# Attention block with a gated unit on one core: order of the first q/k products, pieces of the output weights, engines of the last rows

## The chip, the cores and the metric

The kernel runs on one core of a Trainium2 chip. The metric is the device time of one execution in microseconds; lower is better. The core has a matrix engine (TensorE, PE in the profile, with its weight loads as PEld), VectorE (DVE), ScalarE (ACT), GpSimd (POOL) and SyncE (SP), each with its own instruction stream, executed in order, and 16 DMA engines. Here SP issues nearly all transfers, POOL a few.

## The reference

x is [1, 2048, 576]; there are 32 heads of 18 columns; the gated unit is 4608 wide. All is float32.

```python
xn  = (x - mean(x)) / sqrt(var(x) + 1e-5)
q, k, v = split_heads(xn @ wqkv)                       # 576 -> 3 x 576
s   = (softmax(q @ k.T / sqrt(18)) @ v) @ wo           # heads joined, 576 -> 576
b   = ((xn @ w_gate) * (xn @ w_up)) @ w_down           # 576 -> 4608 -> 576
out = x + s * silu(b)
```

## The kernel before

A float32 operand is split into a high part (a copy in the matrix engine's own 32-bit type, made by ACT) and a low part (operand minus high part, made by DVE or POOL). A product sums high x high, high x low and low x high. The depth of 576 is 4 blocks of 128 and one of 64; in a weight tile the places 0 to 3 and 8 are high, 4 to 7 and 9 are low, and the 64-row rests of high and low share place 8. `PAIRS` lists, for one output bank, the 14 matmuls as (weight place, data place):

```python
PAIRS = ([(i, i) for i in range(4)] + [(i, 4 + i) for i in range(4)]
         + [(8, 8)] + [(4 + i, i) for i in range(4)] + [(9, 8)])
```

In q/k blocks and in the output product the pairs mean different things: in `qk_block` the first number is a piece of the weights and the second one of x; in the output product the first is also a piece of the weights (`wos`), the second one of the transposed attention output (`oT`).

The kernel has three stages. They share one instruction order, which the program writes out by hand.

*Start (to about 200 us).* x comes in chunks of 512 rows. `first_columns` handles chunk 0 tile by tile (128 rows): `norm_stats` and `norm_apply` normalise on DVE (L338 to L349; ACT takes the square root at L340 and copies the last 64 columns at L356), `turn` transposes on TensorE (L400, L401) and ACT writes the high part (L402), `lows` writes the low part on DVE (L406). `w_split` splits the weights: ACT copies (L127), POOL subtracts (L131). POOL's first subtraction is held behind the last `norm_apply` of chunks 0 and 1 by a dependence that the kernel adds (`behind`). Then `qk_block` runs 9 blocks of 128 output columns for each chunk (L441, evicted at L444 and L445), and `v_block` makes v.

*Middle (to about 2530 us).* A planner with costs and due times interleaves the score products (L644, L695), the product with v (L706), the gate and up products (L748) and the down product (L799) on the two halves of the array. It prepares the output weights on the side (`wo_split`, stored to `swo`). When the last gate product is issued, `wo_fetch` loads them: the tile `wos` (places 0 to 7, in a buffer of the x chunks) at L935 and `wos2` (places 8 and 9, in a buffer of the gate weights) at L937.

*End.* For each of 16 tiles of 128 rows: `fetch_o` loads the attention output (`oin`, L1324), `fetch` loads the gate rows (`gin`, L1331, for the first 12 tiles) and x (`xi`, L1333). `join` copies 64 columns on ACT (L1349), `columns` transposes on TensorE (L1357, L1359) and splits with ACT (L1361, L1363) and DVE (L1362, L1364); 28 matmuls make the two halves of the output (L1380); DVE multiplies each half by the gate (L1390), POOL adds x (L1391) and POOL stores the whole tile (L1394). The first four tiles' `oin` are fetched ahead of the loop, then their `gin` and `xi`; tile i + 4 is fetched during tile i. The gate rows of the last four tiles are finished during the loop in small pieces (`chore`; L883 to L893).

SP executes its transfers in order. Each waits for its own buffer to be free and, since eight completion semaphores are used in turn, for the transfer eight places earlier to have landed. In the buffers of the end stage, the second `oin` tile lies where the middle stage kept a tile that the down product reads.

Of the kernel before, what the change touches and what calls it, by code (L numbers as in the profile page):

```python
# [14 lines left out]
try:  # L15
# [5 lines left out]
FT = mybir.dt.float32  # L21
# [3 lines left out]
OP = mybir.AluOpType  # L25
# [4 lines left out]

PAIRS = ([(i, i) for i in range(4)] + [(i, 4 + i) for i in range(4)]
         + [(8, 8)] + [(4 + i, i) for i in range(4)] + [(9, 8)])


def _run(gen):
# [5 lines left out]
def kernel(  # L41
# [10 lines left out]
    nc = tc.nc  # L52
# [26 lines left out]
    swo = dram.tile([128, 10, D], FT, name="swo")  # L79
# [3 lines left out]
    def bank(tag, bufs, k=None):  # L83
        if tag == "g":
            if k is None:
                k = turns[0] = (turns[0] + 1) % 4
            return psum.tile([128, 512], FT, name="pg", tag=f"g{k}", bufs=1)
        return psum.tile([128, 512], FT, name="p" + tag, tag=tag, bufs=bufs)
# [7 lines left out]
    out2 = out.rearrange("o s d -> (o s) d")  # L96
# [246 lines left out]
    def norm_apply(c, t):  # L343
        if t == 0:
            xns[c] = ep.tile([128, 4, 640], FT, name="xn", bufs=1)
        xn = xns[c]
        mv, rs = stat.pop((c, t))
        nc.vector.reciprocal(rs[:, 1:2], rs[:, 0:1])
        op = nc.vector.tensor_scalar(xn[:, t, 0:D], xin[c][:, t, :], mv[:, 0:1], rs[:, 1:2],  # L349
                                     op0=OP.subtract, op1=OP.mult)  # L350
        if c < 2 and t == 3:
            behind.append(op)
        if c:
            nc.vector.tensor_copy(xn[:, t, D:640], xn[:, t, 512:D])
        else:
            nc.scalar.activation(xn[:, t, D:640], xn[:, t, 512:D], AF.Copy)  # L356
# [35 lines left out]
    def first_columns():  # L392

        xc = xcs[0] = pp.tile([128, 9, 512], FR, name="xcx", bufs=2)
        ps, last = {}, bank("a", 2)

        def turn(t):
            ps[t] = bank("g", 3).rearrange("p (k s) -> p k s", k=4)
            for k in range(4):
                nc.tensor.transpose(ps[t][:, k, :], xns[0][:, t, k * 128:(k + 1) * 128], ident)  # L400
            nc.tensor.transpose(last[:, t * 128:(t + 1) * 128], xns[0][:, t, 512:640], ident)  # L401
            nc.scalar.activation(xc[:, 0:4, t * 128:(t + 1) * 128], ps[t], AF.Copy)  # L402

        def lows(t):
            cs = slice(t * 128, (t + 1) * 128)
            nc.vector.tensor_tensor(xc[:, 4:8, cs], ps[t], xc[:, 0:4, cs].bitcast(FT), op=OP.subtract)  # L406

        norm_stats(0, 0)
        norm_stats(0, 1)
        norm_apply(0, 0)  # L410
        norm_stats(0, 2)
        turn(0)
        wq[0], todo = w_split(raws[0], 2)
        for f, a in todo[:2]:
            f(*a, rest=False)
        norm_apply(0, 1)
        norm_stats(0, 3)
        turn(1)
        norm_apply(0, 2)
        lows(0)  # L420
        norm_apply(0, 3)
        for f, a in todo[:2]:
            f(*a, high=False)
        turn(2)
        lows(1)
        turn(3)
        nc.scalar.activation(xc[:, 8, :], last, AF.Copy)
        for f, a in todo[2:]:
            f(*a)
        lows(2)  # L430
        lows(3)
        nc.vector.tensor_tensor(xc[64:128, 8, :], last[64:128, :], xc[64:128, 8, :].bitcast(FT), op=OP.subtract)
        xns.pop(0)


    def qk_block(b, c):
        w = wq[b // 2][:, b % 2]
        p = bank("a" if nqk[0] % 2 else "b", 2)
        nqk[0] += 1
        for n, (a, e) in enumerate(PAIRS):  # L440
            nc.tensor.matmul(p, w[:, a, :], xcs[c][:, e, :], start=n == 0,  # L441
                             stop=n == len(PAIRS) - 1)
        hl = pp.tile([128, 2, 512], FR, name="hl", bufs=3)
        nc.scalar.activation(hl[:, 0, :], p, AF.Copy)  # L444
        nc.vector.tensor_tensor(hl[:, 1, :], p, hl[:, 0, :].bitcast(FT), op=OP.subtract)  # L445
        g0 = blocks[b]
        for kind in range(2):
            lo, hi = max(g0, kind * D), min(g0 + 128, (kind + 1) * D)
            if lo < hi:
                dst = sqk[kind, :, lo - kind * D:hi - kind * D, c * 512:(c + 1) * 512]  # L450
                nc.sync.dma_start(dst.rearrange("h r s -> r h s"), hl[lo - g0:hi - g0].bitcast(FT))
# [149 lines left out]
    n = 8  # L601
# [24 lines left out]
    with ExitStack() as mid:  # L626
# [278 lines left out]
        wos = {}  # L905
# [26 lines left out]

        def wo_fetch():
            wos[0] = xcp.tile([128, 8, D], FR, name="wos", tag="xc")
            nc.sync.dma_start(wos[0].bitcast(FT), swo[:, 0:8, :])  # L935
            wos[1] = wpool.tile([128, 2, D], FR, name="wos2", tag="wgu", bufs=2)
            nc.sync.dma_start(wos[1].bitcast(FT), swo[:, 8:10, :])  # L937

        passed = {}

# [377 lines left out]
    with ExitStack() as end:  # L1318
        ep = end.enter_context(tc.tile_pool(name="end", bufs=1, reuse_waits="tile"))
        oin, gin, xi = {}, {}, {}  # L1320

        def fetch_o(t):
            oin[t] = ep.tile([128, 640], FT, name="oin", bufs=5)
            nc.sync.dma_start(oin[t][:, 0:D], so[t * 128:(t + 1) * 128, :])  # L1324

        def fetch(t):
            rows = slice(t * 128, (t + 1) * 128)
            ready(sdone, t)
            if t < 12:
                gin[t] = ep.tile([128, D], FT, name="gin", bufs=5)  # L1330
                nc.sync.dma_start(gin[t], sg[rows, :])  # L1331
            xi[t] = ep.tile([128, D], FT, name="xi", bufs=5)
            nc.sync.dma_start(xi[t], x2[rows, :])  # L1333

        order = list(range(NT))
        for t in range(12, NT):
            def end_silu(e, t=t):
                gin[t] = e
                sdone.add(t)

            silu(t, lambda: ep.tile([128, D], FT, name="gl", bufs=4), end_silu)
        for t in order[:4]:
            fetch_o(t)
        for t in order[:4]:
            fetch(t)
        oT = {}

        def join(t):
            nc.scalar.activation(oin[t][:, D:640], oin[t][:, 512:D], AF.Copy)  # L1349

        def columns(t):
            o = oin.pop(t)
            oc = ep.tile([128, 9, 128], FR, name="oT", bufs=2)
            oT[t] = oc
            p = bank("b", 2)
            for k in range(4):
                nc.tensor.transpose(p[:, k * 128:(k + 1) * 128], o[:, k * 128:(k + 1) * 128], ident)  # L1357
            p2 = bank("a", 2)
            nc.tensor.transpose(p2[:, 0:128], o[:, 512:640], ident)  # L1359
            pf = p.rearrange("p (k s) -> p k s", k=4)  # L1360
            nc.scalar.activation(oc[:, 0:4, :], pf, AF.Copy)  # L1361
            nc.vector.tensor_tensor(oc[:, 4:8, :], pf, oc[:, 0:4, :].bitcast(FT), op=OP.subtract)  # L1362
            nc.scalar.activation(oc[:, 8, :], p2[:, 0:128], AF.Copy)  # L1363
            nc.vector.tensor_tensor(oc[64:128, 8, :], p2[64:128, 0:128],  # L1364
                                    oc[64:128, 8, :].bitcast(FT), op=OP.subtract)

        join(order[0])
        join(order[1])
        columns(order[0])
        for i, t in enumerate(order):  # L1370
            if i + 2 < NT:
                join(order[i + 2])
            if i + 1 < NT:
                columns(order[i + 1])
            oc = oT.pop(t)
            ps = [bank("g", 3), bank("g", 3)]
            for h in range(2):
                for n, (a, e) in enumerate(PAIRS):
                    w = wos[0][:, a, :] if a < 8 else wos[1][:, a - 8, :]
                    nc.tensor.matmul(ps[h][:, 0:HALF], oc[:, e, :], w[:, h * HALF:(h + 1) * HALF],  # L1380
                                     start=n == 0, stop=n == len(PAIRS) - 1)
            if i + 4 < NT:
                fetch_o(order[i + 4])
                fetch(order[i + 4])
            y = ep.tile([128, D], FT, name="y", bufs=2)
            g = gin.pop(t)
            xt = xi.pop(t)
            for h in range(2):
                cs = slice(h * HALF, (h + 1) * HALF)
                nc.vector.tensor_tensor(y[:, cs], ps[h][:, 0:HALF], g[:, cs], op=OP.mult)  # L1390
                nc.gpsimd.tensor_tensor(y[:, cs], y[:, cs], xt[:, cs], op=OP.add)  # L1391
            for _ in range(3):
                chore()
            nc.gpsimd.dma_start(out2[t * 128:(t + 1) * 128, :], y)  # L1394


# [26 lines left out]
```

## Time and profile before

| what | value |
|---|---|
| median of 3 runs | 2619.4 us (2617.34 to 2620.2) |
| profiled execution | 2617.51 us |
| its span, first to last instruction | 2615.7 us |
| mean granted TensorE clock | 0.999 |
| TensorE, DVE, ACT, POOL busy | 99%, 69%, 60%, 27% |
| DMA moved | 434.30 MB, 166 GB/s |

A timeline row gives the start in us, the time it took, the engine, the line, the operation, the tiles (written <- read), how many instructions were merged into the row, and, in brackets, how long the engine had been idle before it and what ended that. SPq and POOLq are the instruction queues of SP and POOL: there a transfer's row shows its issue, not its transport.

### The profile page before, as it was taken

Reading aid. Unit: us, or ns where it says so; the run is one execution under the profiler, and the core shown is the slowest. Engines: PE = TensorE matmul, PEld = TensorE weight load, DVE = VectorE, ACT = ScalarE, POOL = GpSimd, SP = SyncE. Lnnn points to the kernel's source line nnn. Section 1 sums busy time; section 2 is a strip of 40 time slices with the busy share of each in tenths; the row PEclk is TensorE's granted clock in tenths of the full one; section 3 lists DMA queues with packets and bytes.
Section 4 is the critical chain, followed back from the end, with each engine's and each line's share of the span. In section 5 each row is a group of like instructions: output and inputs, shape, how many; then the busy total and the mean of one; then the engine's idle time right before and its main releaser. Section 6 shows DMA issues by size and latency. Waiting matters only on the chain.

```text
span 2615.7 us, 59267 instructions
## 1 busy us (share of the span) xinstructions
PE 2597.6 (99%) x24504; PEld 2126.2 (81%) x24504; DVE 1797.8 (69%) x2978; ACT 1569.2 (60%) x3125; POOL 696.1 (27%) x738
## 2 busy tenths in 40 slices
PE   8999999999999999999999999999999999999998
PEld 7899888777788878877788788777887788888878
DVE  7209667777777777776777777776777777777336
ACT  4224567666766666666666666665666566666641
POOL 3114444434431222212131222121221222111115
PEclk9999999999999999999999999999999999999999
DMA  7799777676663435564564444444454454443355
GB/s 244 233 296 259 211 205 194 179 192 191 181 184 120 146 134 158 156 168 147 154 164 120 137 146 142 139 134 137 147 168 132 134 151 142 146 134 119 122 188 189
DMA packets 201390, 434.30 MB, mean 166 GB/s; under 512 B 81216, under 2 KB 130784, under 8 KB 167584
## 3 DMA queue, kind: packets, MB, share of 16 engines
q1 hardware_dynamic: 196672, 415.18, 53.1%
q0 software_dynamic: 4448, 15.34, 1.9%
q8 instruction: 192, 3.15, 0.5%
q14 instruction: 78, 0.64, 0.1%
HBM read 314.64 MB, written 110.56 MB: 163 GB/s over the span
## 4 chain that ended last, share of the span: by engine, by line
PE 98%; DMA 1%; DVE 1%; ACT 0%; issue 0%; SPq 0%; POOL 0%; POOLq 0%; ACTq 0%
PE pg L748 35%; PE pg L706 17%; PE pg L799 16%; PE pa L644 11%; PE pb L695 8%; PE pb L441 2%; PE pg L1380 2%; PE pg L498 2%; PE pa L441 2%; DMA xc<-sx 1%; DMA oin<-so 0%; PE pa L695 0%; PE pb L1357 0%; DVE mx L646 0%; PE pg L381 0%; DMA xin<-in_A_x_dram 0%
## 5 line engine op out<-in xcount | busy, mean ns | idle before, releaser
L646 DVE TENSOR_REDUCE mx<-pa 128x1 f32<-128x512 f32 x2016 | 1354.1, 686 | 313.4 <-PE pa L644 181.5
L697 ACT ACTIVATE pt<-pb 128x512 f32<-128x512 f32 x2003 | 1153.9, 601 | 515.5 <-PE pb L695 381.9
L748 PE MATMUL pg<-xc,wgu 64*128 64x512 f32 x7776 | 1389.9, 392 | 0.6 <-DMA xc<-sx 0.5
L748 PEld LDWEIGHTS pg<-xc,wgu 64*128 64x128 f32 x7776 | 1053.2, 186 | 55.2 <-issue 1.7
L799 PE MATMUL pg<-wd,hs 64*128 64x288 f32 x6816 | 823.8, 293 | 0.0
L644 PE MATMUL pa<-ks,qs 54*128 54x512 f32 x2016 | 789.0, 398 | 0.2 <-DVE mx L646 0.2
L799 PEld LDWEIGHTS pg<-wd,hs 64*128 64x128 f32 x6816 | 773.2, 185 | 12.6 <-issue 2.5
L695 PE MATMUL pb<-qs,ks 56*128 56x512 f32 x2003 | 782.7, 398 | 0.0
L706 PE MATMUL pg<-pt,vt 128*32 128x512 f32 x4096 | 459.4, 594 | 1.1 <-ACT st L856 0.6
L644 PEld LDWEIGHTS pa<-ks,qs 54*128 54x128 f32 x2016 | 366.4, 184 | 77.5 <-issue 59.7
L779 POOL TENSOR_TENSOR hs<-us,hs 128x512 fp32r<-128x512 f32 x144 | 186.0, 1292 | 907.8 <-ACT hs L766 658.1
L695 PEld LDWEIGHTS pb<-qs,ks 56*128 56x128 f32 x2003 | 363.4, 184 | 7.6 <-ACT pt L697 0.6
L826 POOL TENSOR_TENSOR acc<-acc,st 128x288 f32<-128x288 f32 x293 | 236.0, 810 | 498.2 <-ACT st L856 255.5
L706 PEld LDWEIGHTS pg<-pt,vt 128*32 128x32 f32 x4096 | 123.3, 110 | 277.4 <-issue 268.6
L712 DVE TENSOR_TENSOR oc<-oc,pg 128x512 f32<-128x512 f32 x64 | 44.0, 687 | 292.6 <-PE pg L706 292.6
L249 POOL TENSOR_TENSOR wgu<-wraw,wgu 128x384 fp32r<-128x384 f32 x108 | 108.4, 1014 | 228.0 <-ACT wgu L248 131.7
L856 ACT ACTIVATE st<-pg 128x288 f32<-128x288 f32 x293 | 120.6, 412 | 25.8 <-PE pg L799 18.7
L862 DVE TENSOR_TENSOR acc<-acc,pg 128x288 f32<-128x288 f32 x252 | 112.7, 448 | 32.5 <-PE pg L799 30.1
L761 DVE TENSOR_TENSOR us<-pg,us 128x512 f32<-128x512 f32 x144 | 98.4, 683 | 27.7 <-PE pg L748 25.4
L754 ACT ACTIVATE us<-pg 128x512 f32<-128x512 f32 x144 | 86.6, 601 | 40.6 <-PE pg L748 26.7
L710 ACT ACTIVATE oc<-pg 128x512 f32<-128x512 f32 x32 | 19.1, 598 | 136.7 <-PE pg L706 136.7
L766 ACT ACTIVATE hs<-us 128x512 fp32r<-128x512 f32 x144 | 90.6, 629 | 12.2 <-DVE us L761 12.0
(128 smaller groups left out, 1266.9 us busy)
## 6 DMA issues: line engine op xcount, KB each, us to landing
wgu<-swg SPq DMA_DIRECT2D x102, 1152.0 KB
wd<-swd SPq DMA_DIRECT2D x50, 1152.0 KB
swg<-wgu SPq DMA_DIRECT2D x36, 1152.0 KB
qs<-sqk SPq DMA_DIRECT2D x192, 144.0 KB
ks<-sqk SPq DMA_DIRECT2D x192, 144.0 KB
swd<-wd SPq DMA_DIRECT2D x18, 1152.0 KB
sqk<-hl SPq DMA_DIRECT2D x32, 512.0 KB
wraw<-in_B_w_up_dram SPq DMA_DIRECT2D x36, 288.0 KB
```

The source lines that it names most:

```text
L249: nc.gpsimd.tensor_tensor(w[:, 9 + b:12 + b, :], raw[:, b:b + 3, :], w[:, b:b + 3, :].bitcast(FT), op=OP.subtract)
L644: nc.tensor.matmul(p, q[rows, t * 128:(t + 1) * 128], k[rows, c * 512:(c + 1) * 512], start=True, stop=True)
L646: nc.vector.tensor_reduce(mx[h][:, t, c:c + 1], p, axis=AX.X, op=OP.max)
L695: nc.tensor.matmul(p, k[rows, t * 128:(t + 1) * 128], q[rows, c * 512:(c + 1) * 512], start=True, stop=True)
L697: nc.scalar.activation(pt[t, c // 2][:, c % 2, :], p, AF.Exp, scale=scale)
L706: nc.tensor.matmul(p[32 * c:32 * c + 32, :], vt[h // 2][:, t, 6 * (h % 2):6 * (h % 2) + 32], pt[t, c // 2][:, c % 2, :], start=t == ts[0], ...
L748: nc.tensor.matmul(ps, gw[n][half[r], a, :], xg[i][half[r], e, :], start=k == 0, stop=k == len(TERMS) - 1)
L779: nc.gpsimd.tensor_tensor(hj[:, 1, :], h32, hj[:, 0, :].bitcast(FT), op=OP.subtract)
L799: op = nc.tensor.matmul(ps[:, 0:HALF], hs[u][half[r], j, a, s * 128:(s + 1) * 128], dw[u][half[r], j, e, i * HALF:(i + 1) * HALF], start=( ...
L826: nc.gpsimd.tensor_tensor(a, a, st, op=OP.add)
L856: nc.scalar.activation(st, ps[:, 0:HALF], AF.Copy)
L862: nc.vector.tensor_tensor(a, a, ps[:, 0:HALF], op=OP.add)
```

## The change

It has three parts. In `qk_block` the pairs are taken in another order: high x high, then low weights x high x, then high weights x low x with the shared place 8, then place 9; and in `first_columns` the last tile is normalised before the first tile's low part is written. The output weights are loaded in three transfers: places 0 to 3 where all were loaded before, then the first two `oin` tiles, then places 8 and 9 and places 4 to 7, then the next two `oin` tiles. For the last tile, DVE adds x to each half and SP stores each half by itself; the other 15 tiles are unchanged. The order of pairs in the output product and in v stays as it is.

```diff
+QK_PAIRS = PAIRS[0:4] + PAIRS[9:13] + PAIRS[4:9] + PAIRS[13:14]
...
         norm_apply(0, 2)
+        norm_apply(0, 3)
         lows(0)
-        norm_apply(0, 3)
...
-        for n, (a, e) in enumerate(PAIRS):
+        for n, (a, e) in enumerate(QK_PAIRS):
             nc.tensor.matmul(p, w[:, a, :], xcs[c][:, e, :], start=n == 0,
-                             stop=n == len(PAIRS) - 1)
+                             stop=n == len(QK_PAIRS) - 1)
...
         def wo_fetch():
             wos[0] = xcp.tile([128, 8, D], FR, name="wos", tag="xc")
-            nc.sync.dma_start(wos[0].bitcast(FT), swo[:, 0:8, :])
+            nc.sync.dma_start(wos[0][:, 0:4, :].bitcast(FT), swo[:, 0:4, :])
             wos[1] = wpool.tile([128, 2, D], FR, name="wos2", tag="wgu", bufs=2)
+
+        def wo_rest():
             nc.sync.dma_start(wos[1].bitcast(FT), swo[:, 8:10, :])
+            nc.sync.dma_start(wos[0][:, 4:8, :].bitcast(FT), swo[:, 4:8, :])
...
-        for t in order[:4]:
+        for t in order[:2]:
+            fetch_o(t)
+        wo_rest()
+        for t in order[2:4]:
             fetch_o(t)
...
-                nc.gpsimd.tensor_tensor(y[:, cs], y[:, cs], xt[:, cs], op=OP.add)
+                if t == order[-1]:
+                    nc.vector.tensor_tensor(y[:, cs], y[:, cs], xt[:, cs], op=OP.add)
+                    nc.sync.dma_start(out2[t * 128:(t + 1) * 128, cs], y[:, cs])
+                else:
+                    nc.gpsimd.tensor_tensor(y[:, cs], y[:, cs], xt[:, cs], op=OP.add)
...
-            nc.gpsimd.dma_start(out2[t * 128:(t + 1) * 128, :], y)
+            if t != order[-1]:
+                nc.gpsimd.dma_start(out2[t * 128:(t + 1) * 128, :], y)
```

## The prediction

> **What bounds the kernel now.** I read the page first (busy shares, the chain that ended last), then the table of busy time by stretch, and last the timelines and waits of the only two places where the chain leaves the matmuls: the first 20 us and everything after 2525 us.
>
> ```profile
> span 2615.7 us, 59267 instructions
> PE 2597.6 (99%) x24504; PEld 2126.2 (81%) x24504; DVE 1797.8 (69%) x2978; ACT 1569.2 (60%) x3125; POOL 696.1 (27%) x738
> ...
> PE 98%; DMA 1%; DVE 1%; ACT 0%; issue 0%; SPq 0%; POOL 0%; POOLq 0%; ACTq 0%
> ...
> 2537.85:2540.42 2.57, 1.50 (x10) 1.05 (x10) 0.47 (x2) 1.05 (x4) 0.00 (x0) 1.00 1.05 406
> ...
> 2610.00:2615.70 5.70, 0.00 (x0) 0.00 (x0) 0.00 (x0) 0.00 (x0) 0.13 (x1) 0.60 0.13 52
> ```
>
> The columns of a stretch are its length, busy us of PE, PEld, DVE, ACT and POOL, the clock, the DMA share and GB/s. TensorE is busy 99% of the span, so an edit pays only where TensorE stands still: the start, the joint ahead of the output product (1.50 busy us of 2.57), and the end, where 5.70 us pass with no compute at all. The built program orders TensorE and ACT as before; only those three places change.
>
> **The start: low weights before low x.** The first q/k block could gain from the new order only if it waited for the low halves of x.
>
> ```profile
> 9.00 0.58 DVE L349 TENSOR_SCALAR xn<-xin,mv,rs 128x576 f32<-128x576 f32 x1
> 9.49 0.68 DVE L406 TENSOR_TENSOR xcx<-pg,xcx 128x512 fp32r<-128x512 f32 x1
> 10.28 0.58 DVE L349 TENSOR_SCALAR xn<-xin,mv,rs 128x576 f32<-128x576 f32 x1
> 10.54 0.42 PE L401 MATMUL pa<-ident,xn 128*128 128x128 f32 x1
> 10.91 1.11 PE L400 MATMUL pg<-ident,xn 128*128 128x128 f32 x4
> 11.00 1.68 POOL L131 TENSOR_TENSOR wgu<-wraw,wgu 128x512 fp32r<-128x512 f32 x2 [9.92 <-DMA xin<-in_A_x_dram]
> 12.06 0.60 ACT L402 ACTIVATE xcx<-pg 128x512 fp32r<-128x512 f32 x1 [0.42 <-PE pg L400]
> 12.71 5.46 PE L441 MATMUL pb<-xcx,wgu 128*128 128x512 f32 x14 [0.47 <-ACT xcx L402]
> ...
> 13.42 0.69 DVE L432 TENSOR_TENSOR xcx<-pa,xcx 64x512 fp32r<-64x512 f32 x1
> ...
> 18.01 3.34 PE L441 MATMUL pa<-xcx,wgu 128*128 128x512 f32 x14
> ...
> L441 PE MATMUL pb<-xcx,wgu 128*128 128x512 f32 x56 | 15.6, 436 | 0.5 <-ACT xcx L402 0.5
> ```
>
> It does not wait for them. Its 14 matmuls take 5.46 us against 3.34 us of the next block, but the group's idle time is the 0.5 us ahead of its first matmul and nothing else (the row that groups 56 of them): a slower pace (5.46 / 14 = 0.39 us each), not a stall. The low weights of this block are done at 11.00 + 1.68 = 12.68 us and the last low x at 13.42 + 0.69 = 14.11 us; the fifth matmul, the first that wants a low half in either order, starts after 12.71 + 4 x 0.39 = 14.3 us. So the order of pairs itself is worth 0, and in later blocks too, since there TensorE has no gap in the timeline. Its cover is this slow pace: were the block fast, it would want low x at 13.6 us and the old order could wait up to 0.5 us.
>
> What pays is the line that moves with it. The last normalisation (L349) now precedes the first low x (L406) on DVE, so it starts at about 9.7 in place of 10.28 us and its rows are ready at 10.3 in place of 10.86. Four transposes take 1.11 us with 0.42 for one alone, so one goes every 0.23 us; after L401 at 10.54 the next could start at 10.77 in place of 10.91, and ACT's copy and the first matmul follow 0.15 to 0.2 us earlier: I take **-0.2 us** (0 if something else holds TensorE there, 0.4 if all of DVE's lead counted). The delayed low x of the first tile ends at about 10.95 us, 3 us before use: 0.
>
> Here a rule of the Trainium skill speaks against even this. TensorE: Matmul & The Clock Gate, Part 1, says that the array runs at half clock until a free-running window of about 3.4 us has been busy, whatever the kernel's start. The trace agrees as far as it goes (0.39 us, then 3.34 / 14 = 0.24 us a matmul); by that rule an earlier start mostly buys 0.2 us at half speed, 0.1 us. What the kernel itself shows of it stands under the rivals.
>
> **The joint: output weights in three pieces.** Before, 2304 + 576 KB of weights stand ahead of the first outputs.
>
> ```profile
> 2526.43 0.34 SPq L935 DMA_DIRECT2D wos<-swo  x1
> 2526.86 0.38 SPq L937 DMA_DIRECT2D wos<-swo  x1
> ...
> 2527.34 0.38 SPq L1324 DMA_DIRECT2D oin<-so  x1
> ...
> 2531.65 1.28 SPq L1324 DMA_DIRECT2D oin<-so  x3
> ...
> SPq L1324 <- PE pg L799: 3.9, 1, 3.9
> ...
> 2539.56 0.33 SPq L1333 DMA_DIRECT2D xi<-in_A_x_dram  x1
> ...
> 2536.75 1.09 PE L799 MATMUL pg<-wdl,hs 64*128 64x288 f32 x7
> 2538.85 0.66 PE L1357 MATMUL pb<-ident,oin 128*128 128x128 f32 x4 [1.00 <-DMA oin<-so]
> ...
> 2539.79 0.58 ACT L1361 ACTIVATE oT<-pb 128x512 fp32r<-128x512 f32 x1
> ...
> 2540.42 4.18 PE L1380 MATMUL pg<-wos,oT 128*128 128x288 f32 x28
> ...
> 2544.44 0.60 PE L1357 MATMUL pb<-ident,oin 128*128 128x128 f32 x4
> ...
> 2545.07 0.60 ACT L1361 ACTIVATE oT<-pb 128x512 fp32r<-128x512 f32 x1 [3.02 <-PE pb L1357]
> ```
>
> TensorE is through at 2537.84 and waits until 2538.85 for the first rows. Then ACT's eviction starts 0.94 us after the transposes, not 0.63 as in the next tile (2545.07 - 2544.44), because the join of the second tile waits for its own DMA ahead of it. With 1152 KB less ahead (2.8 us at the 406 GB/s of the stretch above) the first two tiles land well before 2537.8. Transposes then start about 0.15 us before the last matmul ends (pipelined), at 2537.7; eviction at 2537.7 + 0.63 = 2538.33, its end at 2538.9, first product at 2538.95 in place of 2540.42: **-1.45 us**. The 16 tiles behind it are TensorE-bound, so the gain is kept.
>
> The price is that SP now holds two weight pieces behind the second tile, whose buffer waits 3.9 us for the down product, until 2531.65. They are issued at about 2532.1 and 2532.5. The last piece (low rows 4 to 7) is wanted at the tenth matmul: 2538.95 + 9 x 0.14 + 0.2 (the wait that makes the first tile 4.18 us) = 2540.4. Ahead of and in it stand 1152 + 288 + 288 + 576 + 1152 = 3456 KB, exactly what stood up to the second tile before, and that landed at 2539.56 (the xi row: its lane waits for that landing). So 0.8 us of slack, if the queue does not run dry meanwhile:
>
> ```profile
> 2528.00:2530.00 2.00, 2.00 (x34) 2.00 (x33) 0.91 (x2) 0.00 (x0) 0.00 (x0) 1.00 0.88 157
> 2530.00:2532.00 2.00, 2.00 (x35) 2.00 (x34) 1.29 (x3) 0.00 (x0) 0.00 (x0) 1.00 0.94 369
> 2532.00:2534.00 2.00, 2.00 (x35) 2.00 (x33) 0.98 (x3) 0.00 (x0) 0.00 (x0) 1.00 1.01 424
> ```
>
> By 2532 some 2 x (157 + 369) = 1052 KB are moved, fewer than the 1440 KB of the first two pieces in line: it does not. SP's extra issue costs 0.4 us, hidden under the down product. ACT's join of the third tile waits for its rows until about 2540.3 as before (one tile of 0.7 us behind 2539.56), and tile 1's eviction behind it; that product starts at about 2543.1, so 0. gin, xi and later rows keep their place by bytes: 0.
>
> **The end: DVE adds, SP stores.**
>
> ```profile
> 2605.88 0.56 POOL L1394 DMA_DIRECT2D out_dram<-y  x1 [0.30 <-POOL y L1391]
> ...
> 2607.95 0.46 DVE L1390 TENSOR_TENSOR y<-pg,gl 128x288 f32<-128x288 f32 x1 [1.35 <-PE pg L1380]
> 2608.49 0.79 POOL L1391 TENSOR_TENSOR y<-y,xi 128x288 f32<-128x288 f32 x1 [1.00 <-DVE y L1390]
> 2609.57 0.56 POOL L1394 DMA_DIRECT2D out_dram<-y  x1 [0.30 <-POOL y L1391]
> ...
> L1418 POOLq DRAIN x3: 40/105/5392, 2609.5 to 2615.5; - x3
> ...
> L1418 SPq DRAIN x3: 7/7/7, 2612.3 to 2615.2; - x3
> ...
> DMA to landing us min/median/max: 2.4/3.6/6.3
> ...
> 2523.76 0.46 DVE L724 TENSOR_TENSOR ot<-od,rc 128x288 f32<-128x288 f32 x1
> ```
>
> Two legs close the program. SP has seen the last store at 2612.3; but POOL's drain, which opens with its last store at 2609.55, lasts 5.39 us, to 2614.94, and 0.76 us of closing follow. POOL's leg ends last, by 2.6 us. After the change POOL's last store is that of tile 14: drain from 2605.86 to 2611.25. SP's leg: DVE add 2608.44 to 2608.90 (0.46, the nearest DVE row with both operands outside PSUM), issue at 2608.92, landing 2.05 us later (the least landing of a store is 2.4 us for 288 KB; half of it saves 0.35 at 406 GB/s), SP's own closing 0.35 (2612.3 less the 2609.57 + 2.4 of the old store): 2611.3. Both legs meet, and the span ends at about 2612.05: **-3.65 us**. Bounds: 0.4 less if the half store takes 2.4 us, 0.1 more if POOL's leg is shorter. The adds of the first half lie in DVE's 1.35 us wait.
>
> **Sum.** -0.2 - 1.45 - 3.65 = -5.3 us. The profiled execution took 2617.51 us (span 2615.7 and 1.8 around it) and would be 2612.2; it is 1.9 below the median of the three runs, 2619.4, so the forecast for a median is 2614.1. A difference of 0.2% (5.24 us), about what a measurement of this kernel can tell from no change, lies almost on the sum.
>
> **Rivals.**
> (a) The last weight piece lands late, because the rows queued behind it share the engines: four tiles at 288 / 406 = 0.7 us are 2.9 us, landing at 2542.5, a stall of 2.1 us at the tenth matmul. For it: they are issued within 2 us. Against: landings came in order before. -3.2 us: 2616.2.
> (b) POOL's drain is not tied to POOL's last store but to the last landing of any: 2614.94 lies 2.9 us behind the old landing, so it would end 2611.0 + 2.9 = 2613.9. The end gains 1.05, the whole 2.7: 2616.7. One drain in the trace cannot tell.
> (c) The first block's pace changes at a fixed moment, not after so much work: then 0.2 us earlier buys 0.1, in all 5.2: 2614.2. For it: the pace doubles between two blocks with no change of operands. It is the clock rule cited above.
> (d) Slower: the queue stays at the 157 GB/s of 2528 to 2530 once the pieces are smaller. From 2532 the 2016 KB then take 12.8 us, landing about 2546, a stall of 5.6 at the tenth matmul against 5.3 won: 2619.7. It decides from a landing at 2545.7, and is beyond 0.2% only past 2551. Against: 369 and 424 GB/s right after.
>
> **Chances.** Forecast 0.64, (a) 0.10, (b) 0.12, (c) 0.10, (d) 0.04. About three quarters of the forecast's runs I put beyond 0.2% (medians scatter by more than the 0.06 us between sum and bound, and DVE's part and the drain may both be shorter than priced), and half of (c): faster 0.53. (a), (b) and the rest are the same: 0.43. (d) gives slower 0.04. Range: down to 2612.0, the forecast by a run as low as the lowest before (2617.34, 2.1 below the median); up to 2617.0, which holds (a) and (b).
>
> **What would show it.** Right: the first q/k matmul near 12.5 us; no TensorE gap for oin, and the first product 1.1 us behind the end of the down product in place of 2.6; no wait on wos at the tenth matmul; POOL's drain opening with tile 14's store and the last 5.70 us without compute shrunk to about 3.2. Wrong: a stall inside the first output tile, or a drain that still ends 5 us after the last DVE instruction.

## The result, and the profile after

The changed kernel takes 2615.26 us (median of 19 runs, 2612.65 to 2619.95), the kernel before 2619.68 us on the same chip (19 runs, 2617.34 to 2623.36). The ratio is 0.9984, 95% interval 0.9977 to 0.9991: 4.2 us faster, between 2.4 and 6.0. The forecast was 5.3 us faster, 2614.1 us.

The profiled execution of the changed kernel is one of its slower runs, 2618.19 us with a span of 2616.4, which is 0.7 us longer than the span before. So the two traces can't be compared by their ends; they are compared stretch by stretch. First the page's span and chain:

```profile
span 2616.4 us, 59272 instructions
...
PE 96%; DMA 2%; SPq 1%; DVE 1%; issue 0%; POOL 0%; ACT 0%; ACTq 0%; POOLq 0%
```

The share of DMA in the chain has grown from 1% to 2% and that of SP's queue from 0% to 1%. By line these are a fetch in the start (L531) and the rows of x in the middle (`xc<-sx`), 1% each; the weights of the joint are 0%. The stretches, by the distance between the same matmuls in the two traces (their order is the same):

| stretch | change, us |
|---|---|
| start, to matmul 400 of TensorE's order (84.12 before, 83.78 after) | -0.35 |
| middle, matmul 400 to the last down product | +5.0 |
| joint, last down product to the third tile's transposes (6.88 before, 6.72 after) | -0.16 |
| tiles three to sixteen, to the last multiply on DVE | -0.05 |
| last multiply on DVE to the end of the span (7.79 before, 4.02 after) | -3.8 |

No edit touches the middle but for the fetch of the output weights in its last 11 us, and the 5 us are there before that. Most of them arise at one place, which the timelines of TensorE show; the first row is of the kernel before, the second of the changed one:

```profile
1350.45 0.50 PE L748 MATMUL pg<-xc,wgu 64*128 64x512 f32 x1 [0.51 <-DMA xc<-sx]
```
```profile
1353.50 0.50 PE L749 MATMUL pg<-xc,wgu 64*128 64x512 f32 x1 [2.67 <-DMA xc<-sx]
```

The same matmul waits for the same rows of x, 0.51 us in one execution and 2.67 in the other; with the slower pace that follows, it accounts for 3.7 of the 5 us. In the fourteen traces of this study the 80 matmuls around it (20 before, 60 behind) take from 8.9 to 12.7 us: the longest and the shortest are all kernels with the whole change (this one and e8_warm, then e8b_warm_order and e9_best). So it doesn't go with the edits; it is taken for scatter, and it is why a median of many runs is needed to see 4 us.

**The start.** TensorE's timeline:

```profile
12.49 5.05 PE L442 MATMUL pb<-xcx,wgu 128*128 128x512 f32 x14 [0.47 <-ACT xcx L403]
17.38 3.34 PE L442 MATMUL pa<-xcx,wgu 128*128 128x512 f32 x14
```

The first q/k product starts at 12.49 in place of 12.71 us, the second block at 17.38 in place of 18.01.

**The joint.** The timelines of SP's queue and TensorE, then the one row of the chain that leaves TensorE there (start, length, what), then the table by stretch (length; busy us of PE, PEld, DVE, ACT, POOL; clock; DMA share; GB/s):

```profile
2536.30 0.32 SPq L1328 DMA_DIRECT2D oin<-so  x1
2536.67 0.42 SPq L940 DMA_DIRECT2D wos<-swo  x1
2537.15 0.42 SPq L941 DMA_DIRECT2D wos<-swo  x1
2537.61 1.70 SPq L1328 DMA_DIRECT2D oin<-so  x2
...
2542.43 0.66 PE L1364 MATMUL pb<-ident,oin 128*128 128x128 f32 x4
...
2543.77 1.65 PE L1387 MATMUL pg<-wos,oT 128*128 128x288 f32 x9
2546.30 2.79 PE L1387 MATMUL pg<-wos,oT 128*128 128x288 f32 x19 [0.87 <-DMA wos<-swo]
2548.93 0.60 PE L1364 MATMUL pb<-ident,oin 128*128 128x128 f32 x4
```
```profile
2537.15 9.11 DMA wos<-swo
```
```profile
2531.50:2536.30 4.80, 4.80 (x76) 4.80 (x74) 2.54 (x7) 0.00 (x0) 1.00 (x1) 1.00 0.91 235
2536.30:2540.00 3.70, 3.70 (x60) 3.70 (x58) 2.24 (x5) 0.26 (x1) 0.00 (x0) 1.00 0.85 275
2540.00:2543.00 3.00, 3.00 (x33) 2.83 (x31) 2.09 (x5) 0.26 (x1) 0.00 (x0) 1.00 0.97 323
2543.00:2546.30 3.30, 2.40 (x17) 1.76 (x15) 0.99 (x2) 0.77 (x2) 0.00 (x0) 1.00 0.99 395
```

The wait for the attention rows is gone: the first transpose has no bracket. After nine products of the first tile (x9) TensorE stands still for the rest of the weights. That piece was issued at 2537.15 and landed 9.11 us later, behind what was in line ahead of it, while only 235 to 323 GB/s were moved until 2543. The first product itself comes 1.27 us behind the end of the down product, in place of 2.57; the first tile then takes 1.14 us longer than before, which leaves 0.16. In the kernel before, over the last stretch of the down product, the rate was higher (2537.85 is its end):

```profile
2534.00:2536.00 2.00, 2.00 (x34) 2.00 (x33) 1.31 (x3) 0.00 (x0) 0.00 (x0) 1.00 0.85 345
2536.00:2538.00 2.00, 1.85 (x18) 1.61 (x15) 1.35 (x5) 0.00 (x0) 0.00 (x0) 1.00 1.02 403
```

**The end.** The timeline, and the drains of POOL's and SP's queues (nanoseconds least, median, most; first and last start):

```profile
2610.31 0.56 POOL L1406 DMA_DIRECT2D out_dram<-y  x1 [0.30 <-POOL y L1402]
...
2611.55 2.15 SPq L1400 DMA_DIRECT2D out_dram<-y  x2
2612.39 0.46 DVE L1397 TENSOR_TENSOR y<-pg,gl 128x288 f32<-128x288 f32 x1 [0.86 <-PE pg L1387]
2612.88 0.46 DVE L1399 TENSOR_TENSOR y<-y,xi 128x288 f32<-128x288 f32 x1
...
L1430 POOLq DRAIN  x3: 40/113/5311, 2610.3 to 2616.1; - x3
L1430 SPq DRAIN  x3: 7/7/13, 2615.4 to 2615.9; - x3
```

POOL's long drain now opens with tile 14's store, ahead of the last multiply, and is over at 2610.29 + 5.31 = 2615.60; SP has seen its last store land at 2615.39. The two legs end 0.2 us apart.

### The profile page after: what moved, and what is told of

Its sections match the earlier page's. It is cut to its first block, busy times and chain, and to the rows that moved or that the text cites. A ratio compares the mean times of both kernels' runs of the same rounds, so it can differ in the third digit from the quotient of the medians.

```text
span 2616.4 us, 59272 instructions
## 1 busy us (share of the span) xinstructions
PE 2599.0 (99%) x24504; PEld 2129.3 (81%) x24504; DVE 1799.6 (69%) x2980; ACT 1569.4 (60%) x3125; POOL 693.8 (27%) x735
## 4 chain that ended last, share of the span: by engine, by line
PE 96%; DMA 2%; SPq 1%; DVE 1%; issue 0%; POOL 0%; ACT 0%; ACTq 0%; POOLq 0%
PE pg L749 34%; PE pg L707 17%; PE pg L800 16%; PE pa L645 11%; PE pb L696 9%; PE pg L1387 2%; PE pb L442 2%; PE pa L442 2%; PE pg L499 2%; SPq L531 1%; DMA xc<-sx 1%; DMA wraw<-in_B_w_gate_dram 0%; DMA wos<-swo 0%; PE pa L696 0%; DMA sv<-vo 0%; DMA ks<-sqk 0%
```

## The experiments

Three kernels have one part of the change each (e1 to e3), two have a piece of a part (e5_norm, e10_store); the others change the changed kernel, or add to it. "Before" is each time the kernel before on the same chip.

| kernel | first q/k product, second block | matmul 400 | last down product to third tile's first product | last multiply to end | median (before) |
|---|---|---|---|---|---|
| before | 12.71, 18.01 | 84.12 | 11.60 | 7.79 | 2619.68 |
| changed | 12.49, 17.38 | 83.78 | 11.43 | 4.02 | 2615.26 (2619.68) |
| e1_front | 12.47, 16.76 | 84.62 | 14.09 | 7.80 | 2619.49 (2619.70) |
| e2_joint | 12.86, 17.07 | 85.03 | 11.12 | 7.79 | 2618.78 (2619.70) |
| e3_end | 13.16, 18.66 | 84.75 | 13.42 | 4.01 | 2616.18 (2619.70) |
| e4_rest | 12.46, 17.66 | 83.76 | 14.27 | 4.01 | 2616.32 (2619.70) |
| e5_norm | 12.15, 15.44 | 84.82 | 13.78 | 7.80 | one run |
| e6_last2 | 12.61, 17.57 | 83.68 | 11.40 | 3.71 | one run |
| e7_pass | 12.39, 17.30 | 83.54 | 13.91 | 4.01 | 2615.00 (2619.94) |
| e8_warm | 11.59, 14.87 | 84.43 | 11.22 | 4.02 | 2614.18 (2619.94) |
| e8b_warm_order | 11.68, 15.12 | 84.32 | 10.88 | 4.02 | one run |
| e9_best | 11.73, 15.06 | 83.56 | 10.30 | 3.72 | 2613.64 (2620.68) |
| e10_store | 13.16, 18.12 | 85.59 | 13.26 | 6.88 | one run |
| e11_cold | 12.32, 16.07 | 84.36 | 10.31 | 3.71 | 2613.24 (2619.98) |

All lengths and starts in us, from one trace of each kernel; early transposes added by an experiment are not counted in "matmul 400". The kernels with "one run" have this trace alone.

### Each part alone

```diff
 # e1_front: the kernel before with
+        norm_apply(0, 3)
         lows(0)
-        norm_apply(0, 3)
...
+        for n, (a, e) in enumerate(QK_PAIRS):
```

> The front's edit alone (the fourth normalisation ahead of the first low columns, and the new order of the fourteen q/k products). Theory (the normalisation earns it, the order nothing): the first q/k product starts near 12.5 us in place of 12.71, and from there to the end nothing changes but scatter: 0.2 to 0.6 us under the kernel before, which a time of some 2619 us cannot tell from nothing. Rival (the pace of the first products changes at a moment that the kernel does not set): the first products start at 12.5 too, but the number of slow ones, 9 before and 7 after the whole change, comes out as any number from 6 to 12, so that the second block starts anywhere between 17.1 and 18.4.

Its ratio to before is 0.9998 (0.9989 to 1.0008). The first product is at 12.47 as both expected, but the second block starts at 16.76, a third value: the slow pace ended at 14.93. In the kernels with the old front it ended at 17.31, 15.02, 18.21 and 16.96, in those with the new one at 13.54 to 16.73, and in e5_norm at 11.3, before the block. So the rival is right that the kernel doesn't set the moment, though 16.76 lies below the 17.1 to 18.4 that it gave. Neither reading foresaw where the gain goes; TensorE's waits from 54 to 64 us (us in total, times, longest) show it:

```profile
PE pg L499 <- POOL wv L491: 1.0, 3, 0.4
```

The value product, which follows the q/k blocks, waits for its split weights. TensorE is earlier and stands still there; matmul 400 comes at 84.62, later than in the kernel before, whose slower first block left no wait. Why later is seen under e8_warm.

The joint of this trace is that of the kernel before. It shows that the profile of before was a mild case (TensorE's timeline):

```profile
2542.16 0.66 PE L1358 MATMUL pb<-ident,oin 128*128 128x128 f32 x4 [2.14 <-DMA oin<-so]
...
2543.75 5.52 PE L1381 MATMUL pg<-wos,oT 128*128 128x288 f32 x28
```

The wait for the first rows is 2.14 us, not 1.00, and the first tile behind it takes 5.52, not 4.18 us: fourteen of its products follow each other at 0.24 us in place of 0.13.

```diff
 # e2_joint: the kernel before with wo_fetch cut, wo_rest added, and
+        for t in order[:2]:
+            fetch_o(t)
+        wo_rest()
+        for t in order[2:4]:
```

> The three pieces of the output weights alone. Theory (the last piece is late because it is issued behind SyncE's wait for the second tile's buffer): TensorE no longer waits 1.00 us for the first attention rows, waits 0.9 to 1.2 us for weights at the tenth product of the first tile instead, and from the last product of the down stage to the third tile's transposes it takes 6.4 us in place of 6.6: 0.1 to 0.3 us under the kernel before. Rival (the wait seen after the whole change belongs to that execution alone): no wait at the tenth product, 1.45 us gained as predicted, 5.1 to 5.2 us for the same stretch.

The theory holds, with a smaller wait than it said: none for the attention rows, a gap of 0.84 us from product to product at the tenth, of which TensorE was idle 0.55, and 6.41 us to the third tile's transposes. The row of TensorE's timeline:

```profile
2543.22 2.79 PE L1386 MATMUL pg<-wos,oT 128*128 128x288 f32 x19 [0.55 <-DMA wos<-swo]
```

All five traces with the three pieces in the order of the change and the products of a tile in one pass have that gap, 0.62 to 1.16 us. The time is 0.9 us under before, ratio 0.9997 (0.9988 to 1.0007); the traces say more, though each is of one execution. To the third tile's first product, the five traces with the old joint take 11.60, 14.09, 13.42, 13.78 and 13.26 us (mean 13.2), the five with the new one 11.43, 11.12, 11.40, 11.22 and 10.88 (mean 11.2): 2.0 us gained, and far less scatter.

```diff
 # e3_end: the kernel before with
+                if t == order[-1]:
+                    nc.vector.tensor_tensor(y[:, cs], y[:, cs], xt[:, cs], op=OP.add)
+                    nc.sync.dma_start(out2[t * 128:(t + 1) * 128, cs], y[:, cs])
```

> The last tile's adds on VectorE and its two stores from SyncE, alone. Theory (GpSimd's closing drain starts with GpSimd's own last store and lasts 5.3 us): it starts with the fifteenth tile's store, and from the last multiply on VectorE to the end of the span it takes 4.0 us in place of 7.8: 3.8 us under the kernel before, nearly all of what the whole change gains. Rival (the drain ends a fixed 2.9 us behind the last landing of any transfer): about 2.7 us less of the gain, 1.05 us under the kernel before.

4.01 us in place of 7.79, and 3.5 us under before, ratio 0.9985 (0.9975 to 0.9994). The end alone brings most of what the whole change brings. The rival would have left some 6.7 us there.

### The late weights

```diff
 # e4_rest: the changed kernel with
-        for t in order[:2]:
-            fetch_o(t)
+        fetch_o(order[0])
         wo_rest()
-        for t in order[2:4]:
+        for t in order[1:4]:
```

> The changed kernel with the rest of the output weights fetched before the second tile's attention rows, so that it is not queued behind SyncE's wait for that tile's buffer. Theory (queue order): the rest is issued about 4.6 us earlier, lands near the end of the down stage, TensorE does not wait at the tenth product, and the first tile goes back from 5.2 to 4.0 to 4.2 us between its first product and the third tile's transposes: 1.0 to 1.2 us under the changed kernel. Rival (shared transfer rate: 2 MB cannot land before then whatever the order): the wait stays above 0.5 us at the tenth product, or appears ahead of the second tile's transposes, whose rows now come last, and the stretch stays within 0.4 us of the changed kernel's.

The rival is right about the waits. None is left at the tenth product, and a longer one stands ahead of the second tile's transposes, as TensorE's timeline shows:

```profile
2541.28 0.66 PE L1363 MATMUL pb<-ident,oin 128*128 128x128 f32 x4 [2.38 <-DMA oin<-so]
...
2542.11 5.52 PE L1386 MATMUL pg<-wos,oT 128*128 128x288 f32 x28
```

From the first product to the third tile's transposes it takes 5.35 us, within 0.4 of the changed kernel's 5.16 as the rival said, but the new wait lies ahead of that: the whole stretch is 14.27 us, 2.8 longer than in the changed kernel, and again the tile behind the long wait goes at the slow pace. The median is 3.4 us under before, ratio 0.9987 (0.9978 to 0.9996). In none of the three orders tried (before, changed, this one) were two tiles of rows and all weights there when the down product ended; the order chose who waits, and how long. What can cover it is work that needs neither.

```diff
 # e7_pass: the changed kernel with
+            if i == 0:
+                products(t, oc, 0, 8)
+                products(order[1], oT[order[1]], 0, 8)
+            products(t, oc, 8 if i < 2 else 0, len(PAIRS))
```

> The changed kernel with the output products of the first two tiles in two passes: the eight products that use the first half of the output weights for both halves of both tiles (32 products, about 4.5 us), then the rest. Theory (the rest of the weights is late by its transfer, and work that does not need it covers that): no wait for the weights, and from the last product of the down stage to the end of the second tile's products 1.0 to 1.2 us less than in the changed kernel, 10.7 less about 1.1 us. Rival (the weights come later still, since the rows of the next tiles share the transfers, or the second tile's own columns are late): a wait of 0.5 us or more stays ahead of the second tile's products or of the second pass, and less than half of it is gained.

No wait for weights is left, but the rival's second half came true: the stretch is 13.91 us. TensorE's and ScalarE's timelines:

```profile
2539.96 2.58 PE L1383 MATMUL pg<-wos,oT 128*128 128x288 f32 x16
2544.17 5.70 PE L1383 MATMUL pg<-wos,oT 128*128 128x288 f32 x28 [1.63 <-ACT oT L1368]
```
```profile
2543.38 0.26 ACT L1356 ACTIVATE oin<-oin 128x64 f32<-128x64 f32 x1 [3.30 <-DMA oin<-so]
2543.54 0.58 ACT L1368 ACTIVATE oT<-pb 128x512 fp32r<-128x512 f32 x1
```

On ScalarE the join of the third tile (L1356) stands ahead of the second tile's eviction (L1368) and waits 3.30 us for the third tile's rows. In the old product order nobody needed that eviction yet. Two more kernels move this join behind the second tile's columns (below), and the stretch falls to 10.3 us. The median is 4.9 us under before all the same, ratio 0.9981 (0.9972 to 0.9991), no worse than that of the changed kernel: what one trace shows at the joint need not be what every execution has.

### The start

```diff
 # e8_warm: the changed kernel with, ahead of the first norm_stats,
+        for _ in range(22):
+            nc.tensor.transpose(last[:, 0:128], ident, ident)
```

> The changed kernel with 22 transposes of the identity at the start, from 1.4 to about 6.3 us, where TensorE had nothing to do; nothing reads them. Theory (the pace of the first q/k block depends on how long TensorE has been busy in a window that the kernel does not set): the pace of 0.23 us comes before the block starts, the block takes 3.2 to 3.4 us in place of 4.3 to 5.4, and 1.0 to 1.8 us are gained. Rival 1 (the gaps of 0.3 to 0.7 us between the transposes of x end the fast pace again): the block starts slow as before. Rival 2 (the pace comes a fixed number of slow q/k products after the first): 5 to 12 slow products as in the six traces so far.

TensorE's timeline:

```profile
1.39 4.23 PE L410 MATMUL pa<-ident 128*128 128x128 f32 x22 [1.39 <-DVE ident L102]
...
11.59 3.44 PE L444 MATMUL pb<-xcx,wgu 128*128 128x512 f32 x14 [0.58 <-ACT xcx L403]
14.87 1.29 PE L444 MATMUL pa<-xcx,wgu 128*128 128x512 f32 x5
```

The slow pace ends during the added transposes, the whole first block is fast, and the second block starts 2.5 us earlier than in the changed kernel. The gaps between the transposes of x (up to 0.84 us of idle time) don't bring the slow pace back. And yet in this trace nothing of it arrives at matmul 400. TensorE's waits from 54 to 64 us:

```profile
PE pg L501 <- POOL wv L493: 1.0, 3, 0.4
PE pg L501 <- ACT wv L492: 0.8, 1, 0.8
```

TensorE waits 1.8 us for the value weights, and matmul 400 is at 84.43, 0.65 later than in the changed kernel. ScalarE's timeline shows what holds them:

```profile
53.49 0.60 ACT L447 ACTIVATE hl<-pa 128x512 fp32r<-128x512 f32 x1 [4.61 <-DMA sqk<-hl]
55.82 0.29 ACT L341 ACTIVATE rs<-mv,eps 128x1 f32<-128x1 f32 x1 [1.73 <-DVE mv L340]
56.74 0.29 ACT L341 ACTIVATE rs<-mv,eps 128x1 f32<-128x1 f32 x1 [0.63 <-DVE rs L349]
56.94 1.43 ACT L492 ACTIVATE wv<-wvraw 128x288 fp32r<-128x288 f32 x4
```

Their split (L492) stands in ScalarE's order behind an eviction of q/k (L447), whose buffer is free only when the store of an earlier block has landed, and behind two square roots that wait for DVE. With TensorE earlier, this eviction just waits longer. In the trace of the changed kernel the split begins at 56.20 us, in that of e1_front at 57.10, here at 56.94. In twelve of the fourteen traces matmul 400 comes 27.5 to 27.6 us behind the start of this split; in the kernel before and in e3_end, where the value product itself starts 1.5 us behind it, 27.9 and 27.8. So matmul 400 goes with the split and not with the first block, which begins anywhere from 11.59 to 13.16 us. The median is 5.8 us under before, ratio 0.9980 (0.9970 to 0.9989), not to be told from the changed kernel's 0.9984.

```diff
 # e8b_warm_order: e8_warm with
-QK_PAIRS = PAIRS[0:4] + PAIRS[9:13] + PAIRS[4:9] + PAIRS[13:14]
+QK_PAIRS = PAIRS
```

> The same 22 transposes, and the q/k products in the order of the kernel before (low x before low weights). If the first block is fast, this shows whether the order has a worth that the slow pace hid. Theory (no worth): low x is ready about 13.2 us, and the fifth product starts at about 13.6, so that neither order waits and the block takes the same 3.2 to 3.4 us within 0.1. Rival (the order pays once the block is fast): a wait of 0.1 to 0.5 us inside the first block with the old order and none with the new.

TensorE's timeline:

```profile
11.68 3.61 PE L444 MATMUL pb<-xcx,wgu 128*128 128x512 f32 x14 [0.58 <-ACT xcx L403]
15.12 1.07 PE L444 MATMUL pa<-xcx,wgu 128*128 128x512 f32 x4
```

From block to block 3.44 us against 3.28 with the new order: the fifth product starts 0.1 us late. So, by one trace of each, the new order is worth 0.1 to 0.2 us where the first block starts this early and is fast, at the low end of the rival's range.

```diff
 # e5_norm: the kernel before with
+        norm_apply(0, 3)
         lows(0)
-        norm_apply(0, 3)
```

> The kernel before with only the fourth normalisation moved ahead of the first low columns; the q/k products keep their order. Theory: the move alone brings the first q/k product to 12.4 to 12.6 us, as in the five traces that hold the whole front. Rival (the order of the products has a part in it): it starts at 12.7 us or later, as in the three traces without the move. The joint and the end are those of the kernel before: TensorE waits 1 to 2.3 us for the first attention rows, and where the wait is 2 us or more the next products go at half pace.

The first product is at 12.15 us, 0.25 below the expected range: here the fast pace had come at 11.3 us, during the transposes of x. Until 11.0 these lie within 0.03 us of those of e11_cold, whose first product is at 12.32, so some 0.2 us is the pace's. The move alone brings the products forward, and from 12.15 us on the old order costs nothing even at the fast pace (3.29 us from block to block).

### The drain

```diff
 # e6_last2: the changed kernel with
-                if t == order[-1]:
+                if t in order[-2:]:
...
-            if t != order[-1]:
+            if t not in order[-2:]:
```

> The changed kernel with the last two tiles, not the last one, added on VectorE and stored by SyncE. Theory (GpSimd's drain hangs on GpSimd's own last store): it starts 4.3 us earlier against the last multiply and ends 5.3 us later, well before the last landing; SyncE's leg alone then sets the end, and from the last multiply to the end it takes 3.7 to 3.9 us in place of 4.0. Rival (the drain waits for every transfer of the program): it lasts 9 to 10 us and ends where it did, or moves the end by nothing.

The drains of the two queues:

```profile
L1430 POOLq DRAIN  x3: 40/113/5229, 2603.8 to 2613.6; - x3
L1430 SPq DRAIN  x3: 7/7/13, 2613.0 to 2613.4; - x3
```

POOL's drain opens at 2603.84 and is over at 2609.07, ahead of the last multiply at 2610.19; SP's leg alone sets the end, 3.71 us behind that multiply. So the drain does not wait for the transfers that SP still has to make.

```diff
 # e10_store: the kernel before with
-            nc.gpsimd.dma_start(out2[t * 128:(t + 1) * 128, :], y)
+            (nc.sync if t == order[-1] else nc.gpsimd).dma_start(out2[t * 128:(t + 1) * 128, :], y)
```

> The kernel before with one edit: the last tile's store is issued by SyncE, while GpSimd still does its adds and everything else is as it was. Theory (GpSimd's drain runs from its own last software transfer): the drain is over about 5.3 us behind the fifteenth tile's store, SyncE's leg sets the end, and from the last multiply to the end it takes 4.3 to 4.8 us in place of 7.8. Rival (a closing drain of 5.3 us behind whatever GpSimd does last): it starts with the last add, and the stretch takes 7.0 to 7.4 us.

The timeline of the last rows, and POOL's drain:

```profile
2612.94 0.79 POOL L1391 TENSOR_TENSOR y<-y,xi 128x288 f32<-128x288 f32 x1 [1.00 <-DVE y L1390]
2613.76 0.34 SPq L1394 DMA_DIRECT2D out_dram<-y  x1
...
L1418 POOLq DRAIN  x3: 40/113/5571, 2612.9 to 2619.0; - x3
```

The rival is right, at 6.88 us (0.1 below its range): the drain opens with the last add, though the last software transfer is 2.6 us old by then, and takes 5.57 us with the add's 0.79 in it. So the store alone would have gained 0.9 us, and the edit's 3.8 us need the add to leave GpSimd too.

### All that paid

```diff
 # e9_best: e6_last2 with the 22 transposes, the products of e7_pass, and
+            if 0 < i < NT - 2:
+                join(order[i + 2])
             if i + 1 < NT:
                 columns(order[i + 1])
+            if i == 0:
+                join(order[2])
 # e11_cold: e9_best without the 22 transposes
```

> The changed kernel with the 22 early transposes, the first two tiles' products in two passes with the third tile's join on ScalarE moved behind the second tile's columns, and the last two tiles on VectorE and SyncE. Theory (each stretch adds up): second q/k block 2.0 to 2.5 us earlier than in the changed kernel, no wait over 0.3 us between the first and the third tile's products and the stretch from the last down product to the third tile's last transpose 0.9 to 1.2 us shorter (10.0 to 10.4 us once both tiles' products are done, in place of 11.2), the end 0.1 to 0.3 us shorter: 3.0 to 4.0 us under the changed kernel, near 2612 us. Rival (what is taken away at the joint comes back as another wait, as it did when the third tile's rows held up ScalarE): a gap of 0.8 us or more there and at most 2.5 us in all.

> The kernel of the last run without the 22 early transposes: two passes, the join moved, the last two tiles on VectorE and SyncE. It tells what an earlier start is worth. Theory (the products of the values near 58 us wait for the split value weights, which come at a time of their own, so that a start 2 us earlier is lost there): at the matmul with number 400 TensorE is where it was with the early transposes, within 0.9 us (83.5 to 84.4), and the time is the same within 0.5 us, near 2613.6 on the same chip. Rival (what is gained at the start stays): number 400 comes 1.9 to 2.5 us later than in that run, and so does the end. The joint and the end are as there: 10.2 to 10.4 us from the last down product to the second tile's last product, 3.7 us from the last multiply to the end.

TensorE's timeline of e11_cold at the joint:

```profile
2539.81 6.30 PE L1383 MATMUL pg<-wos,oT 128*128 128x288 f32 x44
```

The 44 products of the first two tiles without a gap, 10.3 us to the third tile's first product, 3.7 us at the end: these are as expected in both. Their medians are 7.0 and 6.7 us under before, ratios 0.9977 (0.9967 to 0.9986) and 0.9973 (0.9962 to 0.9985); the changed kernel's is 0.9984, so both look faster than it, by some 2.5 us, though the intervals overlap and they were not run side by side. Without the early transposes no loss can be seen in the time. Matmul 400 is at 84.36 against 83.56 us, not the 1.9 to 2.5 us later that the rival had; the 0.8 is that of the split of the value weights, which begins at 56.88 against 56.06. The start is limited by the value weights, not by TensorE.

## Why the prediction was right, and where not

**The end, -3.65: right.** Measured -3.8 in the pair and in e3_end. The drain opens with tile 14's store and lasts 5.31 us; both legs meet as worked out. Rival (b) is out by e6_last2. SP's last store landed 2.03 us behind its issue, 2.05 were forecast. One reading was too narrow: the drain follows whatever POOL does last, not its last store (e10_store).

**The joint, -1.45: right in size for the means, wrong in a step, and mis-sized in its base.** The step that failed is "0.8 us of slack" for the last weight piece. It let the piece land at the moment at which the same number of bytes had landed before, 1.7 us behind the end of the down product; it landed 3.76 behind (2537.15 + 9.11 = 2546.26, the last down product ends at 2542.5). The first piece is issued 11.4 us ahead of that end in both traces. From there to the landing the kernel before moved 4.29 MB in 13.1 us (327 GB/s), the changed one 4.45 MB in 15.2 us (293 GB/s), where the step counted 3.5 MB in both: rows of later tiles and the last small stores went through beside the pieces in both. Only 0.16 MB are more than before, some 0.5 us at that rate, so rival (a)'s share is the smaller part of the delay of 2.0 us, and the lower rate the larger.

The queue did not run dry at first, as the step had it (228 GB/s in the first 5.2 us, 218 before). The rate fell behind in the next 6.2 us, the last ones of the down product: 394 to 397 GB/s in the five traces with the old joint, 290 to 333 in the eight in which only the first piece and one tile's rows are issued ahead of SP's wait of about 4 us for the second tile's buffer, 403 in e4_rest, where all three pieces are. So, by that one trace, it goes with the order of issue and not with the size of the pieces; why the transfers issued behind that wait go slower was not tried.

The gap at the tenth product, 0.6 to 1.2 us with the 0.14 that lies between any two, is a quarter to a half of rival (a)'s stall. Rival (d), a queue slowed to 157 GB/s, is out by these rates; its landing "about 2546" should by its own terms read 2544.8 (2532 + 12.8). The base was too kind in turn: the wait removed was 1.00 us in the only profile at hand, and the whole stretch was 1.7 to 2.5 us longer in four others, where the wait is twice as long and the slow pace behind it adds to it. The two errors nearly cancel, which is luck: 2.0 us gained between the means of five traces each, 0.2 in the pair of profiles shown.

**The start, -0.2: right at its place, lost behind it.** The first product came 0.22 us earlier in the pair, by the normalisation, with the order worth nothing there. The block was misread on the way: 5.46 / 14 = 0.39 us is no pace of its own, since in the profile of before its products start 0.43 us apart until the tenth and 0.23 apart from the eleventh, at 17.08 us, on, so the pace doubles inside the first block and not between two; the conclusion that low x is ready in time is not touched. "Its cover is this slow pace" was right too: with the pace fast and the block earlier still, the old order costs 0.1 to 0.2 us. What the step left out is the next limit, the value weights near 58 us, for which neither trace of the pair waits, and eight of the other twelve do. Rival (c) is right in its premise that the moment is not the kernel's: the fast pace comes anywhere from 11.3 to 18.2 us in the eleven traces without early transposes. The Trainium skill (TensorE: Matmul & The Clock Gate, Part 1) has the fast pace come with a free-running window of some 3.4 us. The traces agree that the kernel doesn't set the moment; its spread here, 6.9 us, is wider than one such window.

**The sum.** -5.3 forecast, -4.2 (-6.0 to -2.4) measured. By the traces it is -3.8 for the end, some -2 for the joint in the mean and nothing sure at the start. Which of these the runs fell short in can't be told from an interval 3.6 us wide. The 4.2 us are 0.16%, below the 0.2% that the forecast's sum lay on, so the side to which the chances gave 0.53 (faster by more than that) did not come.

## What to carry to other kernels

At the end of a kernel, look at which queue's closing drain ends last and take the last work, adds as well as stores, off that engine. Where transfers bound a joint, reordering them moves the wait and may shorten it (13.2 to 11.2 us here) or lengthen it (14.3); to remove it, give the matrix engine work that needs the pieces already there, and look at what stands ahead of its operands on the other engines. Before paying for an earlier start, find the next thing that TensorE will meet: here 2.5 us won at 15 us were gone by 62.

## What the runs showed of the hardware

GpSimd's closing drain took 5.23 to 5.57 us in every trace, from the start of the last thing in its stream, while SP's took 0.01. It is 0.08 us shorter for each store that GpSimd has fewer (5.39, 5.31, 5.23). Counted from the end of that last thing it is over 4.8 us later with 16 stores, 4.7 with 15 and 4.6 with 14; e10_store, where that thing is an add of 0.79 us and not the issue of a store of 0.56, has 4.75, like the others with 15.

TensorE fell back to the slow pace after waits of about 2 us: products of 288 columns went from 0.13 to 0.24 us apart for five to sixteen of them behind idle times of 1.6 to 2.4 us, but not behind 0.5 to 1.0. So a long wait was paid for twice here. The same part of the Trainium skill (TensorE: Matmul & The Clock Gate, Part 1) has the slow pace return after an idle window of about 3.4 us; here 1.6 us was enough. At the start, though, with TensorE busy only some 2.5 of the 4 us from 6.3 to 10.3 in e8_warm, the fast pace stayed: idle times of 0.71, 0.84 and 0.38 us, and of 0.58 ahead of the first block, did not bring the slow one back.
